# Row order of w_in, the way of y into feature order, the place of the scores, and one transfer queue, in a gated linear attention kernel with a Mamba output block

## The chip, the core and the metric

The kernel runs on one core of one Trainium2 chip. TensorE (PE in the profile) multiplies matrices; VectorE (DVE), ScalarE (ACT) and GpSimd (POOL) do the elementwise work; SyncE (SP) issues transfers, and its queue is called SPq. ACT and POOL can issue transfers too (ACTq, POOLq). The metric is the time of one execution in device microseconds (us). Over 14 runs the kernel before took 316.13 us in the median, from 313.27 to 319.57 us.

## What is computed

Four batch entries, 8 heads of 48 features and 768 time steps go through a recurrence with a decay for each feature. Its outputs, with the heads side by side (384 features), are projected with w_in to 512 values and 512 gates; the values run through a second recurrence over time, are multiplied with the silu of the gates, and are projected back with w_out.

```python
# first block: q, k, v, alpha of (4, 8, 768, 48)
state = alpha[:, :, t, :, None] * state + einsum('bhd,bhde->bhde'...)   # k[t] outer v[t]
y[:, :, t] = einsum('bhd,bhde->bhe', q[:, :, t], state)
x = y.transpose(0, 2, 1, 3).reshape(4, 768, 384)
# second block
proj = x @ w_in                       # (384, 1024): 512 values, 512 gates
val, gate = proj[..., :512], proj[..., 512:]
h = exp(A_log)[0] * h + val[:, t, :]; ys[:, t, :] = h
out = (silu(gate) * ys) @ w_out       # (512, 384)
```

The weights arrive as 64-bit floats; w_in and w_out are made into 32-bit floats on the chip.

## The kernel before

**Tiling.** The 768 steps of a batch entry are cut into groups of 256 steps, so there are 12 groups (m or n from 0 to 11), each of two chunks (c) of 128 steps. All products are fp32 matmuls on TensorE.

**The attention part of a group m.** `products(m)` makes, on DVE, the running products of alpha (two scans, `prod` and `inv`) and the scaled queries and keys, both in the tile `Z`. For the groups 0 to 2 q, k and alpha are loaded as rows of time ("natural") and transposed on TensorE (`natural_alpha`, `natural_qk`, result `tn`); from group 3 on they are loaded by `load_raw` (12 transfers a group) and transposed on DVE (STREAM_TRANSPOSE). `keys` transposes the keys on TensorE (`tp`, copied to `ktm` by ACT), `scores` multiplies keys with queries (`sc`), `masks` clears what lies in the future (half on DVE; half is copied by ACT and masked by POOL), `values` and `carried` make y from the chunk itself and from the state before it, `state` adds the chunk to the state `st`. `join(m)` moves y from PSUM to the tile `xT`, which has one row for each feature.

**The second block of a group n.** `project(n, cc)` makes 128 values (`pv`) and 128 gates (`pg`) from `xT` and the piece `w_in[cc]`, for cc from 0 to 3. `gated` scans the values on DVE (`hh`), takes the silu of the gates on ACT (`sg`) and multiplies both into `f` (on DVE for n = 0, else on POOL). `output(n)` makes o from the four pieces of `f` and w_out, and stores it.

**Turns.** The loop `for n in range(1, N)` has one turn for each n; in it stand the second block of group n and the attention part of group m = n + 1, while DVE works on products(n + 2), whose pieces are put in by `go`, and SP loads group n + 3. The order of the instructions of each engine is the order of the program text (`manual_schedule`). Ahead of the loop stand groups 0 and 1, the second block of group 0, and the preparation of the weights.

**Weights.** `load_w_in(i)` brings the 64-bit words of piece i to `bits_in`. In `before` the rows of w_in are dealt to the partitions as y lies in PSUM: heads 0 to 3 in partitions 0 to 63, heads 4 to 7 in 64 to 127, 48 rows for each of three of the four heads, and the rows of the fourth head in the 16 partitions left over, so that a piece takes eight transfers of 48 or 16 partitions. `low_word` (ACT), `high_word` (DVE, by the PSUM tiles `bank`) and `word_sum` (POOL) turn a unit of words into fp32. Units 0 to 3 are the pieces of w_in, units 4 and 5 the halves of w_out.

**Transfers and their semaphores.** A transfer issued by SP or ACT is given one of eight semaphores (DMAHW0 to DMAHW7 in the rows below; DMASW0 to 7 for POOL's), and it is issued only when the last transfer that was given the same one has landed. All semaphores are dealt out over SP's and ACT's transfers together. A queue issues its transfers in the order of the program, so one that waits holds all behind it.

**PSUM.** `tp`, `pv`, `pg`, `o` and `tn` of alpha share one ring of three buffers (`mm`); `sc`, `y` and `bank` share two rings of two.

Of the kernel before, what the change touches and what calls it, by code (L numbers as in the profile page):

```python
# [346 lines left out]
def fast(  # L347
# [18 lines left out]
    nc = tc.nc  # L366
# [67 lines left out]


# [6 lines left out]
    def load_w_in(i, engine):  # L442

        for first_row, size in ((0, D), (D, R)):
            for vg in range(2):
                for s in range(2):
                    row, step = (4 * s * D, D) if size == D else ((4 * s + 3) * D, R)
                    cols = ds(2 * (vg * DI + i * C), 2 * C)
                    engine.dma_start(
                        out=bits_in[i][ds(64 * s + first_row, size), :, vg]  # L450
                        .rearrange("p kk n two -> p kk (n two)"),
                        in_=moe_w_in.bitcast(U32)[ds(row, NK * step), cols]
                        .rearrange("(kk p) n -> p kk n", p=step)[0:size])
# [86 lines left out]
    def word_sum(i):  # L540
        w = unit(i)[2].bitcast(I32)
        nc.gpsimd.tensor_tensor(out=w, in0=w, in1=wrs.pop(i), op=ALU.add)  # L542
# [187 lines left out]
    def join(m, engines):  # L730

        y = ys.pop(m)
        xT = xTs[m] = p2.tile([C, 4, GC], FP32, tag="xT", name="xT")
        nc.scalar.activation(xT[:, 1::2], y[1], AF.Copy)
        nc.scalar.activation(xT[:, 0::2], y[0], AF.Copy)

        def transfers():
            for s in range(2):
                for a in range(NK):
                    engines[s].dma_start(out=xT[ds(64 * s + D, R), a], in_=xT[ds(64 * s + R * a, R), 3])  # L740
        return transfers
# [5 lines left out]
    def project(n, cc):  # L747
        g = n % NG
        if cc == 0:
            fs[n] = p1.tile([C, NI, GC], FP32, tag="f", name="f")  # L750
        xT = xTs[n]
        pv = ps_mm.tile([C, GC], FP32, tag="mm", name="pv")
        pg = ps_mm.tile([C, GC], FP32, tag="mm", name="pg")
        for vg, pj in enumerate((pv, pg)):
            for kk in range(NK):
                nc.tensor.matmul(pj, w_in[cc][:, kk, vg, :], xT[:, kk, :],  # L756
                                 start=(kk == 0), stop=(kk == NK - 1))
        return pv, pg

    def gated(n, cc, pv, pg):  # L760
        g = n % NG
        hh = p2.tile([C, GC], FP32, tag=f"h{cc}", name="hh")
        nc.vector.tensor_tensor_scan(  # L763
            out=hh, data0=a_dec[:, cc:cc + 1].to_broadcast([C, GC]), data1=pv,
            initial=prev_h[cc][:, GC - 1:GC] if g else 0.0, op0=ALU.mult, op1=ALU.add)
        prev_h[cc] = hh
        if n == 0:
            nc.scalar.activation(pg, pg, AF.Silu)
            nc.vector.tensor_mul(fs[n][:, cc, :], hh, pg)
# [3 lines left out]
        nc.gpsimd.tensor_mul(fs[n][:, cc, :], sg, hh)  # L773

# [36 lines left out]
    for i in range(2):  # L811
        load_w_out(i, SP)
# [19 lines left out]
    for name in "akq":  # L832
        pair(name, 2, SP, SP)
# [26 lines left out]
    join(0, (nc.gpsimd, nc.gpsimd))()  # L860
# [18 lines left out]
    banks = [ps_sc.tile([C, 4, C], U32, tag=f"sc{i}", name=f"bank{i}") for i in range(2)]  # L879
    pj = project(0, 0)  # L880
    low_word(1)
    high_word(1, banks)
    word_sum(1)
    gated(0, 0, *pj)
    state(1, 0)
    values(1, 0)
    values(1, 1)
    state(1, 1)
    low_word(2)
    high_word(2, banks)  # L890
    word_sum(2)
    carried(1, 0)
    carried(1, 1)
    join(1, (nc.gpsimd, nc.gpsimd))()
    pj = project(0, 1)
    gated(0, 1, *pj)
    low_word(3)
    high_word(3, banks)
    word_sum(3)
    pj = project(0, 2)  # L900
    gated(0, 2, *pj)
    for i in (NI, NI + 1):
        low_word(i)
        high_word(i, banks)
        word_sum(i)
    pj = project(0, 3)
    gated(0, 3, *pj)
    natural_alpha(2)()
    check_alpha(2)
    load_v(2, SP)  # L910
# [7 lines left out]
    for n in range(1, N):  # L918
# [4 lines left out]
        def go(count):  # L923
            for _ in range(count):
                next(steps, None)


        pj = project(n, 0)
        gated(n, 0, *pj)
        if n == 1:  # L930
            k_times, q_times = natural_qk(2, "k"), natural_qk(2, "q")
# [11 lines left out]

# [9 lines left out]
        if n > 1:  # L953
            pj = project(n, 1)
            gated(n, 1, *pj)
        go(1)
        pj = project(n, 2)
        gated(n, 2, *pj)
        go(2)
        if att:  # L960
            state(m, 0)
            values(m, 0)
            values(m, 1)
            state(m, 1)
            carried(m, 0)
            carried(m, 1)
            join(m, (SP, ACT))()
        pj = project(n, 3)
        gated(n, 3, *pj)
# [48 lines left out]
```

## Time and profile before

| | us |
|---|---|
| median of 14 runs | 316.13 |
| lowest, highest | 313.27, 319.57 |
| the profiled execution | 318.35 |
| its span, from the first instruction to the last | 316.62 |
| TensorE busy in the span | 290.9 (92%) |
| DVE busy | 228.3 (72%) |
| POOL busy | 106.3 (34%) |
| ACT busy | 95.9 (30%) |

The profiled execution has 1.7 us around its span and is 2.2 us above the median. In the page's strip of 40 slices a slice is 7.9 us, and a digit is tenths of a slice; "PEclk" is the clock granted to TensorE in tenths. In rows of the timeline and of the chain the first number is the start in us from the start of the span, the second the duration; "x4" counts instructions that were merged into one row, so that its duration takes in the gaps between them. "[... <-X]" is idle time ahead of a row and what ended it. In the windows, a row gives for its stretch the length, then busy us of PE, PEld, DVE, ACT and POOL with counts, the granted clock as a share, the mean busy share of the 16 transfer engines (over 1 where several transfers are counted at once), and GB/s.

### The profile page before, as it was taken

The numbers are of one execution on the slowest core, as the hardware profiler recorded it, in microseconds if no ns is written. First come the engines' busy times: TensorE is split into PE (matmuls) and PEld (weight loads), VectorE is DVE, ScalarE is ACT, GpSimd is POOL, SyncE is SP. The second block draws the span as 40 slices with busy tenths as digits, with TensorE's granted clock in tenths as the row PEclk, the third lists the DMA queues.
The fourth block names the chain that finished last, engine by engine and source line by source line (L and its number), as shares of the span: only waits on it lengthen the run. The fifth ranks groups of instructions, "written<-read, shape, count | busy, mean of one in ns | idle before, by whom it ended". The sixth has DMA issues, their size and how long they took to land.

```text
span 316.6 us, 6042 instructions
## 1 busy us (share of the span) xinstructions
PE 290.9 (92%) x2347; PEld 229.4 (72%) x2347; DVE 228.3 (72%) x263; ACT 95.9 (30%) x198; POOL 106.3 (34%) x103
## 2 busy tenths in 40 slices
PE   6895988999539999999999999999999999999992
PEld 3583766787228868868778788688688688786770
DVE  5994767799506968988988979979889989332110
ACT  4352254132104314224242251242142242221201
POOL 6034375034103305506406018036052164040020
PEclk9999797999958999999999999999999999999999
DMA  9995999920999419529559359189179310100101
GB/s 132 163 171 148 202 277 179 224 93 6 230 212 217 49 56 239 107 87 224 100 139 217 47 156 218 28 216 172 55 184 166 88 24 14 52 0 15 50 5 57
DMA packets 69165, 39.71 MB, mean 125 GB/s; under 512 B 47492, under 2 KB 68616, under 8 KB 69128
## 3 DMA queue, kind: packets, MB, share of 16 engines
q1 hardware_dynamic: 66736, 38.35, 59.3%
q10 hardware_dynamic: 2008, 0.69, 1.1%
q8 instruction: 20, 0.33, 0.5%
q0 software_dynamic: 384, 0.20, 0.3%
q14 instruction: 17, 0.14, 0.2%
HBM read 33.33 MB, written 4.72 MB: 120 GB/s over the span
## 4 chain that ended last, share of the span: by engine, by line
PE 81%; SPq 5%; DMA 4%; issue 4%; POOL 2%; DVE 2%; ACT 1%; DVEq 0%; POOLq 0%; ACTq 0%
PE pv L756 21%; PE o L781 20%; PE pg L756 19%; PE y L704 6%; PE sc L681 6%; SPq L421 4%; PE y L715 3%; PE st L725 3%; DMA v<-in_v_dram 2%; PE tp L671 2%; DMA bits_in<-in_moe_w_in_dram 1%; POOL A L692 1%; POOL w_in L542 1%; SPq L430 1%; DVE w_in L537 1%
## 5 line engine op out<-in xcount | busy, mean ns | idle before, releaser
L773 POOL TENSOR_TENSOR f<-sg,hh 128x256 f32<-128x256 f32 x44 | 54.9, 1247 | 154.5 <-ACT sg L772 135.2
L756 PE MATMUL pv<-xT,w_in 128*128 128x256 f32 x288 | 76.1, 402 | 15.3 <-issue 9.0
L756 PEld LDWEIGHTS pv<-xT,w_in 128*128 128x128 f32 x288 | 54.5, 197 | 29.0 <-issue 11.6
L756 PE MATMUL pg<-xT,w_in 128*128 128x256 f32 x288 | 71.9, 387 | 0.0
L781 PE MATMUL o<-w_out,f 128*128 128x384 f32 x192 | 64.1, 487 | 0.1
L756 PEld LDWEIGHTS pg<-xT,w_in 128*128 128x128 f32 x288 | 56.6, 196 | 8.4
L763 DVE TENSOR_TENSOR_SCAN hh<-a_dec,hh,pv 128x256 f32<-128x256 f32 x32 | 23.4, 731 | 43.4 <-PE pv L756 41.5
L781 PEld LDWEIGHTS o<-w_out,f 128*128 128x128 f32 x192 | 36.3, 190 | 23.1 <-POOL w_out L542 0.3
L772 ACT ACTIVATE sg<-pg 128x256 f32<-128x256 f32 x44 | 16.9, 384 | 106.9 <-PE pg L756 94.3
L692 POOL TENSOR_TENSOR A<-A,mask 128x512 f32<-128x512 f32 x22 | 29.5, 1361 | 28.2 <-ACT A L691 28.2
L635 DVE TENSOR_TENSOR_SCAN prod<-aT,first 128x1024 f32<-128x1024 f32 x12 | 32.9, 2739 | 0.1
L647 DVE TENSOR_TENSOR_SCAN inv<-aT,last 128x1025 f32<-128x1025 f32 x12 | 30.4, 2530 | 0.4
L785 ACT ACTIVATE o_sb<-o 128x384 f32<-128x384 f32 x24 | 11.8, 491 | 47.6 <-PE o L781 47.6
L681 PEld LDWEIGHTS sc<-Z 48*128 48x128 f32 x384 | 22.4, 188 | 3.2 <-issue 2.4
L681 PE MATMUL sc<-Z 48*128 48x128 f32 x384 | 24.7, 278 | 0.0
L704 PE MATMUL y<-A,v 128*64 128x128 f32 x384 | 23.8, 274 | 0.2 <-POOL A L692 0.2
L704 PEld LDWEIGHTS y<-A,v 128*64 128x64 f32 x384 | 20.7, 137 | 0.8 <-POOL A L692 0.7
L693 DVE TENSOR_TENSOR A<-sc,mask 128x512 f32<-128x512 f32 x22 | 15.1, 690 | 6.6 <-PE sc L681 6.4
L626 DVE STREAM_TRANSPOSE aT<-raw_a 128x1024 f32<-128x1024 f32 x9 | 18.3, 2034 | 0.0
L763 DVE TENSOR_TENSOR_SCAN hh<-a_dec,pv 128x256 f32<-128x256 f32 x16 | 10.9, 680 | 10.2 <-PE pv L756 10.2
L626 DVE STREAM_TRANSPOSE Z<-raw_q 128x1024 f32<-128x1024 f32 x9 | 18.3, 2029 | 0.0
L626 DVE STREAM_TRANSPOSE Z<-raw_k 128x1024 f32<-128x1024 f32 x9 | 18.2, 2021 | 0.0
(93 smaller groups left out, 261.0 us busy)
## 6 DMA issues: line engine op xcount, KB each, us to landing
raw_k<-in_k_dram SPq DMA_DIRECT2D x24, 192.0 KB, 5.3
raw_q<-in_q_dram SPq DMA_DIRECT2D x24, 192.0 KB, 5.3
v<-in_v_dram SPq DMA_DIRECT2D x24, 192.0 KB, 4.4
out_dram<-o_sb SPq DMA_DIRECT2D x24, 192.0 KB, 1.9
raw_a<-in_alpha_dram SPq DMA_DIRECT2D x23, 192.0 KB, 3.9
raw_a<-in_alpha_dram SPq DMA_DIRECT2D x18, 176.0 KB, 4.1
raw_k<-in_k_dram SPq DMA_DIRECT2D x18, 176.0 KB, 5.5
raw_q<-in_q_dram SPq DMA_DIRECT2D x18, 176.0 KB, 3.9
```

The costliest lines, as they stand in the source:

```text
L626: nc.vector.transpose(out=to.rearrange("p h (c j) -> p h j c", j=NT), in_=raw_bufs[m % NR][name].rearrange("p h (j d) -> p h j d", d=D)[:, ...
L635: nc.vector.tensor_tensor_scan(out=prod, data0=aT[:, 0:4 * GC], data1=first.rearrange("p h n -> p (h n)"), initial=0.0, op0=ALU.mult, op1= ...
L647: nc.vector.tensor_tensor_scan(out=inv[:, ::-1], data0=aT[:, ::-1], data1=last.rearrange("p h n -> p (h n)")[:, 0:4 * GC + 1][:, ::-1], in ...
L681: nc.tensor.matmul(sc[i][:, p, :], Z[rows, p, 1, cols], Z[rows, p, 0, cols], start=True, stop=True)
L692: nc.gpsimd.tensor_mul(A[:, 1], A[:, 1], mb)
L693: nc.vector.tensor_mul(A[:, 0], sc[0], mb)
L704: nc.tensor.matmul(ys[m][i][ds(64 * s, 64), e, ds(c * C, C)], v_sb[:, c, 2 * p + i, :], A[:, i, p, :], start=(c == 0 and e == 0), stop=Fal ...
L756: nc.tensor.matmul(pj, w_in[cc][:, kk, vg, :], xT[:, kk, :], start=(kk == 0), stop=(kk == NK - 1))
L763: nc.vector.tensor_tensor_scan(out=hh, data0=a_dec[:, cc:cc + 1].to_broadcast([C, GC]), data1=pv, initial=prev_h[cc][:, GC - 1:GC] if g el ...
L772: nc.scalar.activation(sg, pg, AF.Silu)
L773: nc.gpsimd.tensor_mul(fs[n][:, cc, :], sg, hh)
L781: nc.tensor.matmul(os[c], fs[n][:, cc, ds(c * C, C)], w_out[:, cc, :], start=(cc == 0), stop=(cc == NI - 1))
```

## The change

There are five parts.

1. `load_w_in`: the rows of w_in lie in their own order, 128 to a block of `bits_in`. A piece takes two transfers of 128 partitions in place of eight of 48 or 16.
2. `join`: y is copied to a tile `y_sb` (three of the four heads of each half), and transfers of 48, 32 or 16 partitions move it to the rows of its features in `xT`. Heads 0 and 4, which begin at rows 0 and 64 of a block of `xT`, are copied by ACT from PSUM straight into it, so eight transfers are left. Before, y was copied into `xT`, and six transfers of 16 partitions moved the fourth heads.
3. The transfers of `join` in the turns, and that of group 1, are all issued by SP (before: three by SP, three by ACT in the turns; POOL for group 1).
4. In a turn with n > 1, `keys`, `scores` and `masks` of group m stand first, then two blocks of the projection, then the rest of the attention part (`attend`), then the other two blocks. Before, the order was block 0, scores, blocks 1 and 2, attend, block 3.
5. Ahead of the loop: the attention part of group 1 comes before the first projection; w_out is loaded before alpha of group 2; q, k and v of group 2 are loaded after the transfers of group 1's `join`; `gated` is split into `hidden` (scan) and `gate` (silu and product), with a unit of weights between them; `word_sum` does a unit in two halves.

The core of the diff:

```diff
     def load_w_in(i, engine):
-        for first_row, size in ((0, D), (D, R)):
-            for vg in range(2):
-                for s in range(2):
-                    row, step = (4 * s * D, D) if size == D else ((4 * s + 3) * D, R)
...
+        for vg in range(2):
+            engine.dma_start(out=bits_in[i][:, :, vg].rearrange("p kk n two -> p kk (n two)"),
+                             in_=moe_w_in.bitcast(U32)[:, ds(2 * (vg * DI + i * C), 2 * C)]
+                             .rearrange("(kk p) n -> p kk n", p=C))
...
-    def join(m, engines):
+    def join(m, engine):
         y = ys.pop(m)
-        xT = xTs[m] = p2.tile([C, 4, GC], FP32, tag="xT", name="xT")
-        nc.scalar.activation(xT[:, 1::2], y[1], AF.Copy)
-        nc.scalar.activation(xT[:, 0::2], y[0], AF.Copy)
+        y_sb = p2.tile([C, 4, GC], FP32, tag="y_sb", name="y_sb")
+        nc.scalar.activation(y_sb[:, 1::2], y[1], AF.Copy)
+        nc.scalar.activation(y_sb[:, 2], y[0][:, 1], AF.Copy)
+        xT = xTs[m] = p2.tile([C, NK, GC], FP32, tag="xT", name="xT")
         def transfers():
-            for s in range(2):
-                for a in range(NK):
-                    engines[s].dma_start(out=xT[ds(64 * s + D, R), a], in_=xT[ds(64 * s + R * a, R), 3])
+            for h in range(H):
+                s, a = divmod(h, 4)
+                if not a:
+                    kk, row = divmod(h * D, C)
+                    nc.scalar.activation(xT[ds(row, D), kk], y[0][ds(64 * s, D), 0], AF.Copy)
+                    continue
+                d = 0
+                while d < D:
+                    kk, row = divmod(h * D + d, C)
+                    size = min(D - d, C - row)
+                    engine.dma_start(out=xT[ds(row, size), kk], in_=y_sb[ds(64 * s + d, size), a])
+                    d += size
...
+    join(1, SP)()
+    for name in "kq":
+        pair(name, 2, SP, SP)
+    load_v(2, SP)
+    for cc in range(NI):
+        pv, pg = project(0, cc)
+        hidden(0, cc, pv)
+        nc.scalar.activation(pg, pg, AF.Silu)
+        if cc < NI - 1:
+            low_word(cc + 3)
+            words(cc + 3)
+        gate(0, cc, pg)
...
+        def attend():
+            if att:
+                state(m, 0)
...
+                join(m, SP)()
...
         if n > 1:
-            pj = project(n, 1)
-            gated(n, 1, *pj)
+            block(n, 0)
+            go(1)
+            block(n, 1)
+            go(1)
+            attend()
+            go(2)
+            block(n, 2)
...
+        block(n, 3)
```

**SP around the loads of group 4 (turn 1), before.** raw_k_86 and raw_q_85 belong to group 3, raw_a_81 to group 4; the brackets hold the semaphores that a row waits for.

```order
L406 DMA raw_k_86<-in_k_dram 32x4x352 [waits DMAHW2_49]
L406 DMA raw_q_85<-in_q_dram 32x4x384 [waits DMAHW3_49,PE_49,Pool_49]
L406 DMA raw_q_85<-in_q_dram 32x4x352 [waits DMAHW4_49]
L406 DMA raw_q_85<-in_q_dram 32x4x384 [waits DMAHW0_49]
L406 DMA raw_q_85<-in_q_dram 32x4x352 [waits DMAHW1_49]
L786 DMA out_dram<-o_sb 128x384 [waits DMAHW2_49,Activation_49]
L786 DMA out_dram<-o_sb 128x384 [waits DMAHW3_49,Activation_49]
L406 DMA raw_a_81<-in_alpha_dram 32x4x384 [waits DMAHW4_49,DVE_49,PE_49]
L406 DMA raw_a_81<-in_alpha_dram 32x4x352 [waits DMAHW5_49]
L406 DMA raw_a_81<-in_alpha_dram 32x4x384 [waits DMAHW6_49]
L406 DMA raw_a_81<-in_alpha_dram 32x4x352 [waits DMAHW7_49]
```

On SP the semaphores 5, 6 and 7 are left out after 4; three transfers of ACT have them, those of `join(2)`, whose rows on ACT are these:

```order
L728 ACTIVATE S_sb<-st 128x192 [waits PE_49]
L734 ACTIVATE xT<-y_782 128x2x256 [waits DMASW3_49,DMASW2_49,DMASW4_49,DMASW1_49,DMASW5_49,DMASW0_49,PE_49]
L735 ACTIVATE xT<-y_781 128x2x256
L740 DMA xT<-xT 16x256 [waits Activation_49]
L740 DMA xT<-xT 16x256
L740 DMA xT<-xT 16x256 [waits DMAHW7_49]
```

The same place on SP after the change, from the last transfers of group 3's q on; raw_a_81 is again alpha of group 4.

```order
L406 DMA raw_q_85<-in_q_dram 32x4x384 [waits DMAHW3_49,PE_49,Pool_49]
L406 DMA raw_q_85<-in_q_dram 32x4x352 [waits DMAHW4_49]
L406 DMA raw_q_85<-in_q_dram 32x4x384 [waits DMAHW5_49]
L406 DMA raw_q_85<-in_q_dram 32x4x352 [waits DMAHW6_49]
L796 DMA out_dram<-o_sb 128x384 [waits DMAHW7_49,Activation_49]
L796 DMA out_dram<-o_sb 128x384 [waits DMAHW0_49,Activation_49]
L406 DMA raw_a_81<-in_alpha_dram 32x4x384 [waits DMAHW1_49,DVE_49,PE_49]
L406 DMA raw_a_81<-in_alpha_dram 32x4x352 [waits DMAHW2_49]
L406 DMA raw_a_81<-in_alpha_dram 32x4x384 [waits DMAHW3_49]
L406 DMA raw_a_81<-in_alpha_dram 32x4x352 [waits DMAHW4_49]
```

The semaphores now run through without a gap: those that raw_a_81 waits for were last given to SP's own transfers of k and q of group 3.

**TensorE around the start of turn 2, before.** w_in_92 is the last of the four pieces, w_in_89 the first; `o` closes turn 1.

```order
L756 MATMUL pg<-xT,w_in_92 128x256 x3
L781 MATMUL o<-w_out,f 128x384 x8
L756 MATMUL pv<-xT,w_in_89 128x256 x3
L756 MATMUL pg<-xT,w_in_89 128x256 x3
L671 MATMUL tp<-ident,Z 128x128 x8
L681 MATMUL sc_896<-Z 128x128
```

After the change:

```order
L758 MATMUL pg<-xT,w_in_92 128x256 x3
L791 MATMUL o<-w_out,f 128x384 x8
L664 MATMUL tp<-ident,Z 128x128 x8
L674 MATMUL sc_879<-Z 128x128
```

Keys and scores of group 3 (`tp`, `sc`, 16 products of which the first is shown) now stand between the output and the first product that reads the new `xT`; the pieces 89 and 90 follow them.

**DVE at the weights, after the change.** bits_in_96 and bits_in_97 are the words of the third and fourth piece of w_in.

```order
L528 SCALAR_TENSOR_TENSOR w_in_91<-bits_in_96,bank_449 128x3x128
L766 SCALAR_TENSOR_TENSOR hh<-a_dec,pv 128x256
L526 TENSOR_SCALAR bank_448<-bits_in_97 128x384
L528 SCALAR_TENSOR_TENSOR w_in_92<-bits_in_97,bank_448 128x3x128
L526 TENSOR_SCALAR bank_449<-bits_in_97 128x384
L528 SCALAR_TENSOR_TENSOR w_in_92<-bits_in_97,bank_449 128x3x128
L774 TENSOR_TENSOR f<-hh,pg 128x256
L766 SCALAR_TENSOR_TENSOR hh<-a_dec,pv 128x256
L526 TENSOR_SCALAR bank_448<-bits_out 128x384
```

The same place before, from the second piece (bits_in_95) on:

```order
L537 SCALAR_TENSOR_TENSOR w_in_90<-bits_in_95,bank_449 128x3x128
L763 SCALAR_TENSOR_TENSOR hh<-a_dec,pv 128x256
L769 TENSOR_TENSOR f<-hh,pg 128x256
L535 TENSOR_SCALAR bank_448<-bits_in_96 128x384
L537 SCALAR_TENSOR_TENSOR w_in_91<-bits_in_96,bank_448 128x3x128
L535 TENSOR_SCALAR bank_449<-bits_in_96 128x384
L537 SCALAR_TENSOR_TENSOR w_in_91<-bits_in_96,bank_449 128x3x128
L763 SCALAR_TENSOR_TENSOR hh<-a_dec,pv 128x256
L769 TENSOR_TENSOR f<-hh,pg 128x256
L535 TENSOR_SCALAR bank_448<-bits_in_97 128x384
```

Before, scan and product of a block stood side by side, one unit of weights ahead of each; now three pieces of w_in are done before the first scan, and a unit lies between a scan and its product.

More of the change, by code (lines that the diff above doesn't have):

```diff
@@ L831, in fast @@
     k_times, q_times = natural_qk(0, "k"), natural_qk(0, "q")
-    for name in "akq":
-        pair(name, 2, SP, SP)
+    for i in range(2):
+        load_w_out(i, SP)
+    pair("a", 2, SP, SP)
     warm(2)
```

91 lines of the change are left out of this document (34 added, 57 removed).

## The prediction

> **What bounds the kernel.** I read the strip of slices first, then windows over the stretches it sets apart, then the chain that ended last and the transfer queue where it breaks.
>
> ```profile
> PE   6895988999539999999999999999999999999992
> PEclk9999797999958999999999999999999999999999
> ```
>
> TensorE is full from slice 12 (95 us) to the end, and its clock is whole there; holes are only in the first 95 us. The windows show the same:
>
> ```profile
> 59.20:83.28 24.08, 23.81 (x197) 18.84 (x195) 21.99 (x22) 6.65 (x16) 8.20 (x6) 1.00 0.44 109
> 83.28:92.21 8.93, 0.00 (x0) 0.03 (x1) 0.00 (x0) 0.49 (x1) 0.00 (x0) 0.68 1.11 211
> 92.21:97.20 4.99, 4.99 (x13) 3.96 (x14) 2.05 (x2) 0.00 (x0) 0.00 (x0) 0.54 1.03 233
> 116.87:139.48 22.61, 22.61 (x202) 18.39 (x201) 19.20 (x19) 7.45 (x16) 8.99 (x6) 1.00 0.63 141
> 139.48:161.21 21.73, 21.73 (x182) 17.39 (x181) 19.48 (x20) 6.63 (x14) 8.80 (x6) 1.00 0.66 146
> 183.38:294.20 110.82, 110.33 (x944) 88.97 (x944) 82.97 (x93) 34.20 (x73) 39.10 (x30) 1.00 0.46 99
> ```
>
> From turn 3 (116.87) on PE works without a gap: 22.61 of 22.61 us, and 110.33 of 110.82 later. No matmul is taken away, so nothing can be won there. Between 83.28 and 92.21 it does nothing for 8.93 us, and then runs 5 us at 0.54 of its clock.
>
> ```profile
> 78.08 5.17 PE o L781 x16
> 83.28 0.50 ACT o_sb L785
> 83.78 8.44 issue
> 92.21 2.90 PE pv L756 x6
> 95.11 2.18 PE pg L756 x6
> ...
> 116.87 1.29 PE pv L756 x6
> 118.17 1.29 PE pg L756 x6
> 119.46 0.87 PE tp L671 x8
> 120.34 1.99 PE sc L681 x32
> ```
>
> The chain stands between output(1) and block 0 of turn 2, which needs xT of group 2. "issue" says that no engine holds it; the queue of transfers does:
>
> ```profile
> 63.90 15.99 SPq L406 DMA_DIRECT2D raw_a<-in_alpha_dram  x4
> 80.00 1.79 SPq L406 DMA_DIRECT2D raw_k<-in_k_dram  x4
> 81.90 1.79 SPq L406 DMA_DIRECT2D raw_q<-in_q_dram  x4
> 83.74 1.06 SPq L430 DMA_DIRECT2D v<-in_v_dram  x2
> 85.42 4.75 SPq L740 DMA_DIRECT2D xT<-xT  x3
> ```
>
> ```profile
> SPq L406 <- DMA xT<-xT: 14.6, 3, 14.0
> ```
>
> ```profile
> 75.39 0.60 ACT L734 ACTIVATE xT<-y 128x512 f32<-128x512 f32 x1 [2.94 <-PE y L715]
> 75.88 0.59 ACT L735 ACTIVATE xT<-y 128x512 f32<-128x512 f32 x1
> 76.50 1.87 ACTq L740 DMA_DIRECT2D xT<-xT  x3
> ```
>
> Four raw_a transfers took 15.99 us, where four raw_k took 1.79: SP stood 14.0 us for xT transfers. Those are ACT's, issued at 76.50; the rows of the program order show why alpha of group 4 waits for them (semaphores 5, 6, 7). Meanwhile everything behind waits, SP's own xT transfers too: they end at 85.42 + 4.75 = 90.17 and land as PE resumes.
>
> **Part one: the gap of turn 2.** With every transfer on SP, alpha of group 4 waits only for SP's own earlier loads, so the 14.0 us go. What is late next? Three things must be there at turn 2: Z of group 3 (for the scores, now first), xT of group 2, and PE itself. If none is late, the change saves the idle 8.93 us and the slow block: 2.90 + 2.18 against 1.29 + 1.29, **2.50 us**.
>
> On the rule that speaks against this: the Trainium skill, DMA: Bandwidth & Descriptors, section Issuing engines are not separate DMA queues, says that issuing from several engines saves only the sequencer's issue time. By that rule taken alone, leaving ACT's queue could only cost, and these 11.43 us would stay. The 14.0 us row contradicts it here, because the two queues are tied by shared semaphores; the rule stands as the fourth rival.
>
> **Part two: the weights.** Ahead of turn 1 the path runs over words of w_in, DVE, and the products of group 0.
>
> ```profile
> 24.50 4.36 DMA bits_in<-in_moe_w_in_dram
> ```
>
> ```profile
> 18.01 19.91 SPq L449 DMA_DIRECT2D bits_in<-in_moe_w_in_dram  x32
> ```
>
> ```profile
> 24.00:32.00 8.00, 4.32 (x44) 2.96 (x42) 3.89 (x7) 1.89 (x3) 3.65 (x6) 0.99 0.59 151
> 32.00:38.00 6.00, 5.55 (x44) 4.58 (x46) 3.98 (x8) 1.60 (x3) 2.21 (x2) 0.72 0.95 209
> ```
>
> Issuing 32 transfers takes 19.91 us, 0.62 each, while the transfer engines are 0.59 busy at 151 GB/s: 256 GB/s if full, 220 by the second row (209/0.95). A piece is 4 x 144 + 4 x 48 = 768 KB, 3.1 to 3.6 us when data bound, against 8 x 0.62 = 5.0 us of issuing. With two transfers a piece, data decides. The first piece landed at 24.50 + 4.36 = 28.86; it cannot beat the loads ahead of it, the last of which ends at 24.50, nor need it be later than now. I take 27.0, near the middle, and 3.5 us apart for the others: 30.5, 34.0, 37.5, then the halves of w_out at 41.0 and 44.5 (they are as large).
>
> ```profile
> 28.88 0.56 DVE L535 TENSOR_SCALAR w_in<-bits_in 128x768 uint32<-128x768 uint32 x1 [4.08 <-DMA bits_in<-in_moe_w_in_dram]
> 30.35 2.48 DVE L689 TENSOR_TENSOR A<-sc,mask 128x512 f32<-128x512 f32 x4
> 32.75 0.55 DVE L535 TENSOR_SCALAR bank<-bits_in 128x384 uint32<-128x384 uint32 x1
> 34.39 0.55 DVE L537 SCALAR_TENSOR_TENSOR w_in<-bits_in,bank 128x384 uint32<-128x384 uint32 x1
> 35.41 0.69 DVE L763 TENSOR_TENSOR_SCAN hh<-a_dec,pv 128x256 f32<-128x256 f32 x1 [0.47 <-PE pv L756]
> 53.35 0.42 DVE L769 TENSOR_TENSOR f<-hh,pg 128x256 f32<-128x256 f32 x1 [1.05 <-ACT pg L768]
> 54.65 0.17 DVE L632 TENSOR_TENSOR first<-aT,prod 128x4 f32<-128x4 f32 x1 [0.88 <-ACT aT L590]
> 81.94 1.22 DVE L658 TENSOR_TENSOR Z<-Z,prod 128x1024 f32<-128x1024 f32 x1
> ```
>
> A unit costs DVE 34.39 + 0.55 - 32.75 = 2.2 us, a scan 0.7, a product 0.4. In the new order: piece 0 at 27.0 and masks from 28.5 to 31.0; unit 1 to 33.2; unit 2 from 34.0 to 36.2; scan 0 to 36.9; unit 3 from 37.5 to 39.7; product 0 and scan 1 to 40.8; unit 4 from 41.0 to 43.2; product 1 and scan 2 to 44.3; unit 5 from 44.5 to 46.7; product 2, scan 3, product 3 to **48.2**. Before, the last product ended at 53.35 + 0.42 = 53.77. I win **5.6 us** for what follows: output(0), and DVE's work to Z of group 3. PE has slack here: a block is 1.29 + 1.29 = 2.6 us and DVE's three steps between blocks are 3.3. The half sums on POOL let `pv` begin before all of a unit is summed; DVE's chain hides that. Bounds: if words land no sooner than now, the last piece at about 41 (18.01 + 19.91, plus about 3), every step from unit 3 on is some 3.5 us later and 2.1 us are left; if the first piece came with the loads ahead of it (24.50) and DVE waited for no other, 2.5 + 1.8 = 4.3 more would go, 9.9 together.
>
> From `first` to the end of Z(3) DVE took 81.94 + 1.22 - 54.65 = 28.5 us nearly without a pause (21.99 busy of 24.08 in the first window). Only one scan of a block moves ahead of a scan of products. So Z(3) ends at 83.16 - 5.6 = 77.6, and output(1) at 83.25 - 5.6 = 77.7: scores after the key transposes, which need less than Z, start without waiting.
>
> **Part three: xT of group 2.** Block 0 now stands behind keys (0.87) and scores (2.0): needed at 77.7 + 2.9 = 80.6. SP must issue 12 raw loads, two of v and eight of xT. Before, from raw_k on, 8 raw, 2 v and 3 xT took 90.17 - 80.00 = 10.2 us; four more raw at 1.79 and five xT at 0.62 (ACT's three took 1.87) make 15.1, and landing 1.8, 16.9 together.
>
> ```profile
> xT<-xT SPq DMA_DIRECT2D x30, 16.0 KB, 1.8
> ```
>
> They start behind the store of output(0). At the earliest that is 63.90 - 5.6 = 58.3, at the latest 63.90: done at 75.2 to 80.8. Nor can it be before y: ACT's copies end at about 75.39 + 0.6 + 1.2 - 5.6 = 71.6 (0.6 more than now: two wide copies become one wide, one of half width and two of 48 rows), eight issues and a landing later 78.2. So it fits with 0 to 2 us to spare, to within 0.2; I count 0.
>
> **The turns.** Keys and scores at the head, blocks two and two: the sum of PE is the same. Queue: SP's xT transfers rise from three to eight, 3.0 us more issuing; they start behind `carried`, 13 us ahead of the next block 0 (two blocks 5.2, output 5.2, keys and scores 2.9), and need 8 x 0.62 + 1.8 = 6.8 plus 1.8 of copies. Hidden; if that cover went, it would cost up to what is over. Loads behind a waiting xT transfer are those of the next turn, which wait for the output anyway. Scores need Z at the turn's head:
>
> ```profile
> 136.86 1.23 DVE L658 TENSOR_TENSOR Z<-Z,prod 128x1024 f32<-128x1024 f32 x1
> ```
>
> Z ends at 138.09, 1.4 us ahead of the turn's end at 139.48, though today it is asked for only after block 0. In the new order the scan of products waits for block 0's scan and no longer for block 1's, so Z should end no later: cost 0.
>
> **Sum**, in the profiled execution's own time: 318.35 - 8.93 - 2.50 - 5.6 = 301.3. That execution is 2.2 us above the median of 316.13. If the 2.2 us lie in work that stays, the median becomes 299.1; if they lie in the gap, 301.3. I take 300.
>
> **Rivals.**
> (1) *xT of group 2 is late after all.* k, q and v of group 2 now stand behind group 1's eight transfers, so loads of group 4 may start later than 63.90. Three us later makes 83.7 against 80.6: 3.1 us of gap, and the slow clock's 2.5 with it: 300 + 5.6 = 305.6. For it: 24 transfers a turn share one queue. Against: w_in's issuing falls by 24 x 0.62 = 15 us.
> (2) *The words come no sooner.* 2.1 in place of 5.6: 303.5. For it: the transfer engines are already 0.95 busy from 32 us on.
> (3) *Z is late in every turn.* Each turn then waits at its head. There are nine such turns (2 to 10); from 16/9 = 1.8 us a turn on the change is slower than before. DVE would have to end Z 1.8 us past the turn's end, 3.2 later than at 138.09. At 3 us it is 300 + 27 = 327. For it: DVE is 19.2 to 19.5 busy of 22 us, and its scans lengthen beside POOL. Against: the order above, and the checks of the weights, which stand behind Z.
> (4) *The queue still stands.* If alpha of group 4 waits for something else at about 79 us, only the head is won: 318.35 - 5.6 = 312.8, about 311.5 by the median.
>
> **Chances.** Forecast 0.55, (1) 0.17, (2) 0.12, (3) 0.07, (4) 0.09. The range takes in the forecast with its bounds (a head that wins 4.3 us more: 295.7, rounded to 295), (1) and (2): 295 to 308; (4) and most of (3) stay out. A measurement here tells about 0.5% (1.6 us) from no change: faster 0.92, within 0.03 and slower 0.05, the last two out of (3).
>
> **What would show it.** raw_a of group 4 in one row of about 2 us; no "issue" over 2 us in the chain near 80; w_in issued in under 10 us; DVE's last product of group 0 near 48 and Z(3) near 78; clock whole from 80 us on; turns of 21.7 to 22.6. Wrong it is if TensorE waits at each head for DVE's Z, or block 0 of turn 2 for transfers.

## The result, and the profile after

The changed kernel takes **301.79 us** in the median of 10 runs (300.06 to 304.73). The kernel before took 316.16 us in 47 runs beside it (312.94 to 319.6). The ratio is 0.956 (95% interval 0.952 to 0.959). The profiled execution took 301.61 us with a span of 299.9.

The strip of slices of the changed kernel, 7.5 us a slice; the last row is what the transfer engines moved:

```profile
PE   8899999999699999999999999999999999999991
PEclk9999999999999999999999999999999999999998
GB/s 129 163 176 313 340 92 169 230 264 188 115 235 122 177 225 62 158 225 67 179 215 56 163 223 65 185 207 56 192 214 45 107 13 31 52 15 26 52 5 60
```

Behind the first two slices the strip of before had holes (digits 5, 8, 8, 5 and 3 in the first 95 us); here one 6 is left, at 75 to 82 us, and the clock is 0.9 or more up to the last slice. SP's queue of the changed kernel (start, duration, what was issued, how often):

```profile
18.06 7.09 SPq L442 DMA_DIRECT2D bits_in<-in_moe_w_in_dram  x8
58.78 2.55 SPq L406 DMA_DIRECT2D raw_a<-in_alpha_dram  x4
61.97 2.73 SPq L406 DMA_DIRECT2D raw_k<-in_k_dram  x4
65.36 2.64 SPq L406 DMA_DIRECT2D raw_q<-in_q_dram  x4
68.48 1.08 SPq L430 DMA_DIRECT2D v<-in_v_dram  x2
70.13 9.14 SPq L742 DMA_DIRECT2D xT<-y_sb  x8
```

Alpha of group 4 takes 2.55 us where it took 15.99; w_in is issued in 7.09 us where it took 19.91. But the eight transfers of xT take 9.14 us, 1.1 each. TensorE at the end of turn 1 and the start of turn 2, in the same run:

```profile
68.84 5.32 PE L791 MATMUL o<-w_out,f 128*128 128x384 f32 x16
74.00 1.04 PE L664 MATMUL tp<-ident,Z 128*128 128x128 f32 x8
74.97 2.06 PE L674 MATMUL sc<-Z 48*128 48x128 f32 x32
76.96 0.70 PE L758 MATMUL pv<-xT,w_in 128*128 128x256 f32 x2
78.75 0.67 PE L758 MATMUL pv<-xT,w_in 128*128 128x256 f32 x2 [1.10 <-DMA xT<-y_sb]
80.80 0.67 PE L758 MATMUL pv<-xT,w_in 128*128 128x256 f32 x2 [1.37 <-DMA xT<-y_sb]
```

Scores start without a wait. Block 0 needs xT at 76.96; its first piece is there, the other two are late by 1.10 and 1.37 us, **2.5 us** together. DVE in the same run:

```profile
25.49 0.55 DVE L526 TENSOR_SCALAR w_in<-bits_in 128x768 uint32<-128x768 uint32 x1
44.73 0.42 DVE L774 TENSOR_TENSOR f<-hh,pg 128x256 f32<-128x256 f32 x1
73.59 1.23 DVE L651 TENSOR_TENSOR Z<-Z,prod 128x1024 f32<-128x1024 f32 x1
```

The words of the first piece are taken at 25.49 without a wait, the last product of group 0 ends at 45.15 (before: 53.77), Z(3) at 74.82, just ahead of the scores at 74.97.

Where the time went is read best from the starts of the output products, since every turn ends with one. The two profiled executions differ by 16.7 us of span: output(0) starts at 45.30 in place of 53.92 (8.62); from there to output(1) it is 23.54 in place of 24.00 (0.46); to output(2) 25.13 in place of 33.63 (8.50); from there to output(11) 194.09 in place of 193.74 (0.35 lost); the rest 11.82 in place of 11.33 (0.49 lost). The medians differ by 14.4: before's profiled execution was 2.2 above its median, and the table below shows its head late.

### The profile page after: what moved, and what is told of

Its sections match the earlier page's. It is cut to its first block, busy times and chain, and to the rows that moved or that the text cites. A ratio compares the mean times of both kernels' runs of the same rounds, so it can differ in the third digit from the quotient of the medians.

```text
span 299.9 us, 6112 instructions
## 1 busy us (share of the span) xinstructions
PE 286.8 (96%) x2347; PEld 226.4 (75%) x2347; DVE 226.1 (75%) x263; ACT 100.4 (33%) x222; POOL 106.6 (36%) x105
## 4 chain that ended last, share of the span: by engine, by line
PE 87%; DVE 6%; SPq 1%; issue 1%; ACT 1%; DMA 1%; POOL 0%; POOLq 0%; DVEq 0%; ACTq 0%
PE pv L758 21%; PE o L791 21%; PE pg L758 19%; PE y L697 7%; PE sc L674 7%; PE st L718 4%; PE y L708 4%; PE tp L664 2%; PE warm L827 2%; SPq L742 1%; PE tn L596 1%; PE tn L577 1%; DVE bank L526 1%; DVE prod L628 1%; DVE Z L602 1%
## 5 line engine op out<-in xcount | busy, mean ns | idle before, releaser
L778 POOL TENSOR_TENSOR f<-sg,hh 128x256 f32<-128x256 f32 x44 | 57.2, 1300 | 107.0 <-ACT sg L777 63.9
L758 PE MATMUL pv<-xT,w_in 128*128 128x256 f32 x288 | 72.9, 388 | 2.5 <-DMA xT<-y_sb 2.5
L758 PE MATMUL pg<-xT,w_in 128*128 128x256 f32 x288 | 70.2, 380 | 0.0
L758 PEld LDWEIGHTS pv<-xT,w_in 128*128 128x128 f32 x288 | 52.6, 190 | 13.6 <-issue 4.1
L758 PEld LDWEIGHTS pg<-xT,w_in 128*128 128x128 f32 x288 | 54.6, 190 | 7.9 <-DVE hh L766 0.5
L685 POOL TENSOR_TENSOR A<-A,mask 128x512 f32<-128x512 f32 x22 | 28.0, 1292 | 67.0 <-ACT A L684 67.0
L718 PEld LDWEIGHTS st<-v,ktm 128*64 128x64 f32 x320 | 11.4, 137 | 3.9 <-issue 3.3
```

What stands on the lines that cost most here:

```text
L685: nc.gpsimd.tensor_mul(A[:, 1], A[:, 1], mb)
L718: nc.tensor.matmul(st[ds(64 * i, 64), p, :], ktms[c][:, p, i, :], vs[m % NV][:, c, 2 * p + i, 0:D], start=(ch == 0 and p == 0), stop=(ch = ...
L758: nc.tensor.matmul(pj, w_in[cc][:, kk, vg, :], xT[:, kk, :], start=(kk == 0), stop=(kk == NK - 1))
```

## The experiments

All ten runs in one table; the medians of the kernel before beside them were 316.07 to 316.86. "Head" is the start of output(0), "1 to 2" the way from output(1) to output(2), "2 to 11" from output(2) to output(11), all in the profiled execution, in us.

| kernel | time | ratio, 95% interval | head | 1 to 2 | 2 to 11 |
|---|---|---|---|---|---|
| before | 316.16 | | 53.92 | 33.63 | 193.74 |
| changed | 301.79 | 0.956 [0.952, 0.959] | 45.30 | 25.13 | 194.09 |
| e1 before, one queue | 304.86 | 0.963 [0.956, 0.971] | 52.09 | 22.17 | 193.75 |
| e7 before, second half by POOL | 304.75 | 0.965 [0.958, 0.972] | 50.98 | 22.17 | 193.75 |
| e2 changed, two queues | 305.35 | 0.969 [0.961, 0.976] | 44.42 | 30.61 | 194.10 |
| e3 changed, block 0 first | 305.57 | 0.969 [0.962, 0.976] | 44.50 | 29.23 | 193.75 |
| e4 changed, w_in in 32 transfers | 307.48 | 0.973 [0.965, 0.982] | 48.95 | 25.72 | 194.10 |
| e9 changed, rows dealt as before | 304.53 | 0.961 [0.953, 0.968] | 50.38 | 23.82 | 194.10 |
| e6 row order, old program order | 308.75 | 0.976 [0.970, 0.983] | 55.83 | 22.17 | 193.75 |
| e5 changed, v behind xT | 298.61 | 0.945 [0.940, 0.950] | 45.06 | 22.29 | 194.11 |
| e8 as e5, old later turns | 298.51 | 0.945 [0.940, 0.950] | 45.05 | 22.30 | 193.75 |
| e10 changed, group 1 by POOL | 298.73 | 0.944 [0.936, 0.951] | 44.48 | 22.31 | 194.10 |

The head of one and the same program varies: that of before, which e1 and e7 share, from 50.98 to 53.92 (mean 52.3), that of the changed kernel, which e2, e3, e5 and e8 share, from 44.42 to 45.30 (mean 44.9). TensorE's clock has a part in it: in the strip of slices (PEclk) before and e1 have two slices at 0.7 among the first seven, e7 one, the changed kernel none. The other two columns repeat within 0.02 us where the program is the same.

### The queue of turn 2: e1, e7 and e2

e1 changes one word of the kernel before:

```diff
-            join(m, (SP, ACT))()
+            join(m, (SP, SP))()
```

> The kernel before, with only the transfers of join in the turns moved from SP and ACT to SP alone (six transfers, old layout, old order of the turn). Theory (shared semaphores: alpha of group 4 waited 14.0 us for ACT's transfers): the wait goes, the loads of group 4 are issued from 64 us on, y is copied at 76.5, six transfers at 0.6 and a landing end near 82 to 83, when output(1) ends; the gap of 8.9 us and the slow block's 2.5 us go: about 305 us (304 to 308). Rival (it is the scores at the head of a turn that hide the transfers): a gap of 5 us or more stays at turn 2, 311 us or more.

SP's queue in e1, at alpha of group 4 and at xT of group 2:

```profile
60.71 2.54 SPq L406 DMA_DIRECT2D raw_a<-in_alpha_dram  x4
74.60 3.77 SPq L740 DMA_DIRECT2D xT<-xT  x6
```

Alpha takes 2.54 us, and output(2) follows 22.17 us behind output(1): 33.63 - 22.17 = 11.46 us less, against 8.93 + 2.50 = 11.43 in the prediction. The time falls by 11.6 us against the runs of before beside it (median 316.45). One queue alone is thus most of the whole change.

e7 keeps two queues, but the second half goes by POOL, whose transfers have semaphores of their own:

```diff
-            join(m, (SP, ACT))()
+            join(m, (SP, nc.gpsimd))()
```

> The kernel before, with the three transfers of the second half of y issued by POOL in the turns in place of ACT: two queues still, but POOL's transfers have semaphores of their own (DMASW). Theory (it is the semaphores that SP's and ACT's transfers share, not the number of queues, that made SP stand 14.0 us): alpha of group 4 takes 2 to 3 us on SP, the gap of turn 2 goes or falls under 3 us, and the time is 304 to 308, close to the 304.9 of one queue alone; POOL's part may be late by some us where POOL is in the middle of other work, at most about 3 us in turn 2. Rival (two queues are slower as such, or ACT's issuing was the cost only by its place): SP still stands over 8 us at alpha of group 4, and the time is 311 or more.

```profile
60.53 2.43 SPq L406 DMA_DIRECT2D raw_a<-in_alpha_dram  x4
```

SP's row in e7 is as short as with one queue, and "1 to 2" is the same 22.17. So the number of queues does not matter here; that SP and ACT draw on the same eight semaphores does.

e2 puts that back into the changed kernel:

```diff
-    def join(m, engine):
+    def join(m, engine, other=None):
...
-                    engine.dma_start(out=xT[ds(row, size), kk], in_=y_sb[ds(64 * s + d, size), a])
+                    (other if other and s else engine).dma_start(out=xT[ds(row, size), kk], in_=y_sb[ds(64 * s + d, size), a])
...
-                join(m, SP)()
+                join(m, SP, ACT)()
```

> The changed kernel, with the transfers of heads 5 to 7 issued by ACT again in the turns (four by SP, four by ACT). Theory (shared semaphores): alpha of group 4 again waits for transfers of ACT, which cannot be issued before y of group 2 is copied at 68 us; SP stands some 10 us, xT of group 2 is complete near 86 in place of 80.7, and TensorE idles about 8 us and is slow behind it: about 310 us (307 to 314). Rival (two queues cost nothing, they only save issuing): 302 us or less, since SP issues four transfers fewer in each turn.

SP's queue at alpha of group 4, SP's row of waits over the whole execution (us in all, times, longest) and TensorE at turn 2, in e2:

```profile
61.50 7.83 SPq L406 DMA_DIRECT2D raw_a<-in_alpha_dram  x4
```

```profile
SPq L406 <- DMA xT<-y_sb: 43.5, 17, 5.7
```

```profile
82.71 2.90 PE L758 MATMUL pv<-xT,w_in 128*128 128x256 f32 x6 [6.56 <-DMA xT<-y_sb]
```

Alpha again waits for ACT's transfers of xT, 5.7 us at the longest, and block 0 is 6.56 us late and then slow. The mechanism returns, at 5.5 us over the changed kernel (30.61 - 25.13) and 8.3 over e5, where xT is in time; the 11.5 of before it does not reach, and the time is 305.4, under the 307 to 314 that I had expected.

### The head of the program: e4, e6 and e9

e4 leaves the layout of the changed kernel and cuts each of the two transfers of a piece into four of 32 partitions:

```diff
-            engine.dma_start(out=bits_in[i][:, :, vg].rearrange("p kk n two -> p kk (n two)"),
...
+            for part in range(4):
+                rows = ds(32 * part, 32)
+                engine.dma_start(out=bits_in[i][rows, :, vg].rearrange("p kk n two -> p kk (n two)"),
...
```

> The changed kernel, with each piece of w_in brought by eight transfers of 32 partitions in place of two of 128 (same bytes, same layout). Theory (issuing bound the weights): 32 issues at 0.62 us take about 20 us again, the last piece lands near 41 and DVE's unit 3 starts there in place of 35.5: 5.5 us later, about 307 us (304 to 309). Rival (the order of the work around the weights brought the head's gain, not the number of transfers): 302 us as the changed kernel.

The windows from 24 to 38 us (PE, PEld, DVE, ACT and POOL busy, clock, share of the transfer engines, GB/s), first of the changed kernel, then of e4:

```profile
24.00:32.00 8.00, 7.69 (x110) 6.07 (x108) 7.84 (x14) 3.05 (x5) 6.84 (x11) 1.00 1.00 311
32.00:38.00 6.00, 6.00 (x58) 4.97 (x55) 4.82 (x11) 3.81 (x8) 3.15 (x4) 1.00 1.12 336
```

```profile
24.00:32.00 8.00, 7.38 (x92) 5.19 (x90) 4.74 (x8) 2.08 (x4) 4.85 (x8) 1.00 0.73 195
32.00:38.00 6.00, 4.89 (x63) 4.29 (x64) 4.87 (x9) 4.02 (x9) 3.67 (x4) 1.00 0.71 199
```

DVE at the first and the fourth piece of w_in in e4:

```profile
27.13 0.56 DVE L528 TENSOR_SCALAR w_in<-bits_in 128x768 uint32<-128x768 uint32 x1 [2.31 <-DMA bits_in<-in_moe_w_in_dram]
39.08 0.56 DVE L528 TENSOR_SCALAR bank<-bits_in 128x384 uint32<-128x384 uint32 x1 [1.24 <-DMA bits_in<-in_moe_w_in_dram]
```

With 32 issues the transfers of this stretch (w_in's and those behind them) move 195 to 199 GB/s in all with the engines 0.7 busy, and DVE waits for words at each piece; with eight they move 311 to 336, and it never waits for words. The head is 4.1 us later than the mean of the changed kernel (48.95 - 44.9).

e6 has the row order and one queue in the turns, but the old order of the program ahead of the loop and in the turns; groups 0 and 1 stay with POOL, as before. It is the kernel before with load_w_in and join as the change has them, and:

```diff
-            join(m, (SP, ACT))()
+            join(m, (SP, SP))()
```

> The kernel before with one queue (SP) for the transfers of y and with the row order of w_in and of y (parts 1 to 3 of the change), but with the old order ahead of the loop and in the turns (parts 4 and 5 left out). It splits the 6.9 us by which output(0) starts sooner in the changed kernel (45.3) than with one queue alone (52.3). Theory (issuing gives about half, the order of the weights' units and of group 1 the rest): output(0) starts at 48 to 50.5, and the time is 303.5 to 307, since xT of group 2 needs eight issues in place of six and block 0 stands first. Rival (the layout alone gives all, the order nothing): output(0) starts at 45 to 47. Other rival (the layout gives nothing without the order, since the old path runs over group 1 and not over the words): 51.5 or later, and 305 or more.

TensorE and POOL in e6, at group 0 and at the last piece of w_in:

```profile
30.25 0.67 PE L759 MATMUL pv<-xT,w_in 128*128 128x256 f32 x2 [1.37 <-DMA xT<-y_sb]
32.82 0.67 PE L759 MATMUL pv<-xT,w_in 128*128 128x256 f32 x2 [1.90 <-DMA xT<-y_sb]
...
49.67 1.56 PE L759 MATMUL pv<-xT,w_in 128*128 128x256 f32 x6 [2.94 <-POOL w_in L535]
```

```profile
43.76 4.02 POOL L742 DMA_DIRECT2D xT<-y_sb  x8
47.80 1.82 POOL L535 TENSOR_TENSOR w_in<-w_in,wr 128x768 int32<-128x768 int32 x1
```

I had expected the head at 48 to 50.5; it came at 55.83, 3.5 us later than the mean of before and 1.9 later than the latest of its three, as the rival had it by which the layout gives nothing without the order. In the old order block 0 of group 0 stands right behind its xT, whose eight transfers are late, and POOL issues those of group 1 for 4.02 us between two sums of words, so that the last piece is 2.94 us late.

DVE in e6 takes the words of the first piece as early as in the changed kernel, but then stands at scan and product of block 0:

```profile
25.47 0.55 DVE L528 TENSOR_SCALAR w_in<-bits_in 128x768 uint32<-128x768 uint32 x1
34.70 0.69 DVE L766 TENSOR_TENSOR_SCAN hh<-a_dec,pv 128x256 f32<-128x256 f32 x1 [3.03 <-PE pv L759]
37.71 0.42 DVE L772 TENSOR_TENSOR f<-hh,pg 128x256 f32<-128x256 f32 x1 [2.32 <-ACT pg L771]
```

Over the four blocks such waits for TensorE and ACT come to 10.1 us, and there is none for words.

e9 is the fourth corner: the changed order and one queue, with load_w_in and join of before, so 32 transfers for w_in and six for xT, SP's from group 1 on:

```diff
-                    engines[s].dma_start(out=xT[ds(64 * s + D, R), a], in_=xT[ds(64 * s + R * a, R), 3])
+                    engine.dma_start(out=xT[ds(64 * s + D, R), a], in_=xT[ds(64 * s + R * a, R), 3])
```

> The changed kernel with the rows of w_in dealt as before (32 transfers for w_in, six transfers and two wide copies for y), and with the changed order ahead of the loop and in the turns, and one queue: the fourth corner beside one queue alone (output(0) at 52.3), the row order with the old program order (55.8) and both (45.3). Theory (the old program order put the word sums of POOL and the issuing of 32 transfers in line; the new order alone wins 3 us or so, and fewer issues another 3.7 on top of it): output(0) at 48 to 50, near the 49.0 of the run with 32 issues and eight transfers for y; output(2) 22.2 to 24 us behind output(1), since six transfers of y are shorter than eight; time 301.5 to 305. Rival (the row order and the program order win only together): output(0) at 51.5 or later, time 305 or more. Other rival (the order does it all): output(0) at 46.5 or sooner.

DVE at the first piece of w_in in e9:

```profile
28.45 0.56 DVE L533 TENSOR_SCALAR w_in<-bits_in 128x768 uint32<-128x768 uint32 x1 [3.17 <-DMA bits_in<-in_moe_w_in_dram]
```

The head comes at 50.38, just behind the 48 to 50 that I gave; the rival by which the two win only together gave 51.5 or later. The order alone gives 1.9 us (52.3 - 50.38, no more than the head of one program varies), the row order alone takes 3.5, and both together give 7.4 (52.3 - 44.9). The sum of the two alone is a loss, so in this the rival was right. The waits of DVE show why: with the new order and the old rows (e9) it stands 5.8 us for words of w_in (3.17, 0.55, 1.58 and 0.50 at the four pieces), with the old order and the new rows (e6) not at all. Only in the new order are the words the path, and only then does it pay that they come faster. The clock is a part that no run sets apart: in the strips the old order has slow slices in the head (two in e6 too), the new order none (changed, e4 and e9). Nor does a run tell the steps of the order from each other.

### Block 0 of turn 2, and the later turns: e3, e5, e8 and e10

e3 puts block 0 at the head of every turn from n = 2 on, as before the change, and the rest in the old order:

```diff
+        else:
+            block(n, 0)
...
-            block(n, 0)
-            go(1)
             block(n, 1)
```

> The changed kernel, with the old order in the turns from 2 on: block 0, scores, blocks 1 and 2, attend, block 3. Theory (the scores at the head give eight transfers on one queue the time that they need): turn 2 waits for xT from 74.2 to 80.7, 6.5 us in place of 2.5, with a slow clock behind it (2.5), and in each later turn y to the last landing takes 8.4 to 10.9 us while only 8.0 us of work stand in between: 0.4 to 2.9 us a turn, ten turns. 302 + 6.5 + 4 to 29: 312 to 337 us. Rival (the order does not matter, the gain is the queue's and the weights'): 302 to 306 us.

TensorE at turn 2 in e3:

```profile
75.22 0.67 PE L758 MATMUL pv<-xT,w_in 128*128 128x256 f32 x2 [1.85 <-DMA xT<-y_sb]
76.67 1.19 PE L758 MATMUL pv<-xT,w_in 128*128 128x256 f32 x2 [0.79 <-DMA xT<-y_sb]
78.72 1.19 PE L758 MATMUL pv<-xT,w_in 128*128 128x256 f32 x2 [0.86 <-DMA xT<-y_sb]
79.70 2.77 PE L758 MATMUL pg<-xT,w_in 128*128 128x256 f32 x6
```

Turn 2 is 4.1 us longer (29.23 against 25.13): waits of 3.5 us, and matmuls at half speed. The later turns, which I had expected to lose 4 to 29 us, are 0.35 us shorter in all; the time, 305.57, lies under the 312 to 337 that I gave, and where the rival had it (302 to 306). Keys and scores at the head are worth something in turn 2 alone.

e5 asks why xT of group 2 is late. It moves the two transfers of v of group 3 behind those of xT:

```diff
-        if n + 2 < N:
+        if n > 1 and n + 2 < N:
             load_v(n + 2, SP)
...
             attend()
+            load_v(n + 2, SP)
```

> The changed kernel, with one step moved: in turn 1 the two transfers of v of group 3 are issued behind the eight transfers of xT of group 2, not ahead of them (they are wanted only later in turn 2). Theory (xT of group 2 is late because its eight issues stand behind v and behind the backlog of the raw loads): the issues start about 1.6 us sooner and find less ahead of them, the two waits of 1.10 and 1.37 us in block 0 of turn 2 go or fall below 1 us together, output(2) starts 23 us or less behind output(1) instead of 25.1, and the time is 299.3 to 300.3. Rival (the bytes of all the loads behind each other set the landing, whatever is issued first): the waits stay at 2 to 2.5 us and the time at 301.8, within 0.5 us. Also possible: v itself becomes late in turn 2, and 1 us or more is lost there.

SP's queue and TensorE at turn 2 in e5:

```profile
65.71 2.66 SPq L406 DMA_DIRECT2D raw_q<-in_q_dram  x4
68.89 5.63 SPq L742 DMA_DIRECT2D xT<-y_sb  x8
74.57 1.21 SPq L430 DMA_DIRECT2D v<-in_v_dram  x2
```

```profile
74.73 2.06 PE L674 MATMUL sc<-Z 48*128 48x128 f32 x32
76.72 1.56 PE L758 MATMUL pv<-xT,w_in 128*128 128x256 f32 x6
```

xT's issues start 1.24 us sooner and end at 74.52 in place of 79.27; block 0 starts without a wait, "1 to 2" is 22.29, and the time is **298.61 us**, below both kernels and below what I had expected.

e8 adds the old order for the turns from 3 on:

```diff
+        elif n > 2:
+            block(n, 0)
```

> As the run before, and from turn 3 on the order of a turn is the old one (block 0, scores, blocks 1 and 2, the rest of the attention part, block 3); turn 2 keeps keys and scores first. Theory (the head of a turn helps only in turn 2; in the later turns it costs the 0.36 us by which output(2) to output(11) grew, through a wait of 0.13 us in every third turn): output(2) to output(11) takes 193.7 as before, and the time is 0.2 to 0.5 us under the run before, 298.9 to 300. Rival (the later turns need scores ahead of block 0, since the eight transfers of xT land later than the six did): every later turn loses 0.3 us or more, 302.5 or more.

The 0.36 us of the later turns come back in the trace (194.11 to 193.75), as expected, but the medians (298.51 and 298.61) don't tell the two apart, and the time is a little under the 298.9 to 300 that I had given.

e10 gives group 1's transfers ahead of the loop back to POOL:

```diff
-    join(1, SP)()
+    join(1, nc.gpsimd)()
```

> The changed kernel with the eight transfers of xT of group 1 issued by POOL, as before the change, in place of SP. Theory (in the run with the row order and the old program order POOL stood 4.0 us at these issues between two word sums, and the last piece of w_in came late by that; it is the place of POOL's issuing in the chain of words that costs): the sums of units behind them come up to 4 us later, DVE's chain hides some of it, and output(0) starts 1 to 4 us later than 45.3; q and k of group 2 and with them the loads of group 4 no longer stand behind the eight transfers on SP, so that xT of group 2 is in time and up to 2.5 us come back at turn 2: 300 to 304. Rival (POOL has slack enough in the new order): output(0) within 0.5 us of 45.3, and the time 299 to 300, under that of the changed kernel.

SP's queue in e10, POOL at group 1, and TensorE at block 0 of turn 2:

```profile
55.78 2.46 SPq L406 DMA_DIRECT2D raw_a<-in_alpha_dram  x4
64.02 1.21 SPq L430 DMA_DIRECT2D v<-in_v_dram  x2
66.11 7.41 SPq L742 DMA_DIRECT2D xT<-y_sb  x8
```

```profile
35.28 4.02 POOL L742 DMA_DIRECT2D xT<-y_sb  x8
39.31 1.97 POOL L535 TENSOR_TENSOR w_in<-w_in,wr 128x384 int32<-128x384 int32 x2
```

```profile
76.13 1.56 PE L758 MATMUL pv<-xT,w_in 128*128 128x256 f32 x6
```

My theory fell on one half: POOL does stand 4.02 us at the issues, but in the new order the sums behind them are hidden, and the head (44.48) is no later. The other half held: SP issues its loads 3 to 4.5 us sooner (alpha of group 4 at 55.78 in place of 58.78, v at 64.02 in place of 68.48), block 0 does not wait, and the time is 298.73 us, under the 300 to 304 that I had given. The same 3 us are won as in e5. So xT of group 2 is late only with both ahead of it on SP, group 1's eight transfers and v of group 3: taking away either is enough.

## Why the prediction was right

I predicted 300.0 us, from 295 to 308; it is 301.8. The steps one by one:

- **The gap of turn 2** (11.43 us): right in mechanism and size, 11.46 in e1. That it was the shared semaphores, not the second queue as such, is shown by e7; the fourth rival, by which the queue would still stand, is out. The Trainium skill's rule (DMA: Bandwidth & Descriptors, section Issuing engines are not separate DMA queues) agrees with e7 in so far as a second queue bought nothing there ("1 to 2" is 22.17 with one and with two); as a forecast for this change, with the 11.43 us staying, it is contradicted by e1.
- **The weights** (5.6 us, bounds 2.1 to 9.9): the mechanism was right, the term mis-sized. It measured 8.6 between the two profiled executions and 7.4 between the means of runs with the same head. What was mis-sized is when the words come: I had them at 27.0 and then 3.5 us apart, from a rate of 220 to 256 GB/s for full transfer engines. In the row order 311 to 336 GB/s were moved; DVE took the first words at 25.49, 1.5 us sooner, and waited for no others, so that its way to the last product took 19.7 us (25.49 to 45.15) in place of 21.2 (27.0 to 48.2). These two, 3.0 us, are the error. That the rate was low because I had read it where narrow transfers ran is likely (e4, with 32 partitions, gives 195/0.73 = 267), but was not tried by itself. Of the 8.6 us, some 1.6 were before's own head, late in that execution (53.92 against a mean of 52.3). The second rival (words no sooner) is out by the 25.49, against 28.88 before; e4, where the words are later, shows what they are worth, 4.1.
- **xT of group 2** (0 us, "0 to 2 us to spare"): wrong; TensorE waits 2.5 us, and with block 0 in three pieces "1 to 2" is 2.8 us over e5 and e10. Two things failed. The need came sooner, at 76.96 in place of 80.6, since the head won more. And the issue prices, taken from a quiet stretch (1.79 for four raw loads, 0.62 for one of xT), did not hold behind a full queue: from the start of alpha of group 4 the way was 5.4 us for twelve raw loads by my sum and 9.2 in the trace (58.78 to 68.00), 5.0 for eight of xT and 9.14 in the trace. For the raw loads the view of waits says why: between 60 and 70 us SP's raw loads stood 3.4 us in seven waits for earlier raw loads of its own queue to land, each at most 0.6 us. A single queue is held by its semaphores too, only for less. What held the transfers of xT stays open (last section). The start itself, 58.3 at the earliest, was met within 0.5. The first rival named a cause (loads of group 2 behind group 1's transfers), and e10 shows that without it xT is in time. But its way was another: it had the loads of group 4 start later than 63.90, and they started at 58.78; and the slow clock that I had priced with it at 2.5 did not come.
- **The turns** (0): 0.35 us lost over nine turns, and e3 and e8 win it back. The third rival, Z late in every turn, did not come.
- **Frame**: 301.3 in the profiled execution's time, and 299.1 if its 2.2 us over the median stayed. In the trace it is 318.35 - 11.43 - 8.62 - 0.46 + 2.9 + 0.35 + 0.5 = 301.6, where 2.9 is what was lost again at turn 2 (11.43 - 8.50). The 3.0 us that the head won beyond my sum and the 2.9 lost at turn 2 cancel. That the total is nearer than its terms is luck. Two figures of the prediction don't add up, and nothing hangs on them: 0.03 and 0.05 are more than the third rival's 0.07, out of which they are to come; and the fourth rival's 312.8 is 310.5 if the 2.2 us are taken off, not 311.5.

## What to carry to other kernels

Where transfers of two engines draw on one small set of semaphores, a transfer that waits for its data can hold loads on the other engine that have nothing to do with it; look which semaphores a standing row waits for before counting queues. Put what is wanted next ahead of what is wanted later in a queue: two transfers of v moved behind xT, or eight of group 1 moved to an engine with slack, were worth 3 us after the large gap was gone. And a layout that cost 3.5 us alone and an order that won 1.9 won 7.4 together, so such parts are tried in all four combinations.

## What was not expected of the hardware

The time that SP needs to issue the same transfers differs with what stands ahead of them. Eight transfers of xT took 9.14 us right behind v in the changed kernel and 5.63 in e5, where v stood behind them. The difference lies in the first of the eight, which held SP for 3.80 us in the changed kernel, with no semaphore named for it and y copied since 67.8; in e5 none of the eight took more than 0.59:

```profile
70.13 3.80 SPq L742 DMA_DIRECT2D xT<-y_sb  x1
```

What held it was not tried by itself. The 7.41 us of e10 can't be set beside these: there SP came to the first transfer at 66.11, before ACT had copied y (67.0), and the view of waits names ACT for 2.7 us.

The granted clock of TensorE survived two waits of 1.10 and 1.37 us with 0.67 us of work between them (changed kernel, clock 1.00 in every 2 us from 76 to 86), but not waits of 1.85 and 0.79 us, again with 0.67 us between them (e3):

```profile
73.20:76.00 2.80, 0.84 (x3) 0.30 (x2) 0.81 (x1) 0.54 (x2) 0.00 (x0) 1.00 0.27 62
76.00:78.00 2.00, 1.19 (x2) 0.50 (x2) 0.00 (x0) 0.00 (x0) 0.00 (x0) 0.66 0.24 59
78.00:80.00 2.00, 1.28 (x3) 1.13 (x4) 0.05 (x1) 0.00 (x0) 0.00 (x0) 0.50 0.82 237
80.00:82.00 2.00, 2.00 (x6) 1.55 (x6) 2.00 (x2) 0.00 (x0) 0.00 (x0) 0.50 0.99 249
```

A mean of 0.66 from 76 to 78 us puts the fall to 0.50 at about 76.6, some 3.3 us after the first wait began (75.22 - 1.85 = 73.37) and near the end of the second; the third wait of e3 (0.86 us) came when the clock was low already. It stays low for 6.83 us, to 83.48, while TensorE is full again from 79.7 on. The Trainium skill (TensorE: Matmul & The Clock Gate, section What's actually happening) tells of a free-running window of about 3.4 us after which an idle array is slowed. The lengths agree: inside the turns and the head, every slow stretch in the traces here lasted 3.41 us (e1, e6, e7), 6.83 (e2, e3) or 3.41 and 10.24 (before). But the array need not be idle for all of such a window: in the 3.4 us up to the fall in e3 TensorE had worked 0.84 us. The changed kernel worked no more than 0.94 us in the 3.4 us from 77.66 on and kept its clock, so what share of idle time decides, and from where it is counted, is left open.
